# An attention stage that loads Q and K nine tokens to a partition, turns them with 64x64 products, and spreads its reciprocals by two transfers

## The chip, the cores and the metric

The kernel runs on one core of a Trainium2 chip. The metric is device time in microseconds (us) of one execution. The core has five engines that work side by side and meet through semaphores: PE (TensorE, the matrix engine; its loads of stationary operands are listed apart as PEld), DVE (VectorE), ACT (ScalarE), POOL (GpSimd) and SP (SyncE, which here only issues transfers). Transfers between DRAM and on-chip memory (DMAs) run on 16 DMA engines. Each engine takes its own instructions in the order in which the program wrote them.

## The reference

A forgetting attention over 4 batches of 8 heads, 576 tokens and 64 dimensions feeds two gated feed-forward layers.

```python
B, H, S, D = q.shape                       # 4, 8, 576, 64
scores = matmul(q, k^T) / sqrt(D)
cum    = cumsum(maximum(s, 0))             # one number per head and token
scores = where(causal, -1e9, scores + minimum(-(cum[i] - cum[j]), 0))
attn   = softmax(scores)                   # rows of 576 keys
x      = (attn @ v), heads joined          # 2304 tokens x 512
x      = (sigmoid(x @ w_gate) * (x @ w_val)) @ w_out      # 512 -> 1536 -> 512
h      = x @ w_in                                          # 512 -> 2048
out    = (h * cos(h)) @ w_out2                             # 2048 -> 512
```

The weights of the feed-forward layers come in 64-bit floats, which the kernel unpacks with integer operations into a high and a low 32-bit part (`wp`).

## The kernel before, in words

**Stages.** `attention()` handles 16 pairs of heads, `moe()` the two feed-forward layers. The attention leaves its result in `XH` and `XL` (a high and a low part). The feed-forward layers are three products for each one (`mm3`, lines 355 to 357) in an unbroken stream on PE, and `moe()` starts its own tiles in memory that the attention gave back, so its first gating waits for the attention's last user.

**One pair, p.** The names below are those of the order table.

- `GQp`, `GKp` (line 515) load Q and K. Two transfers per operand, one for each head: 512 of the 576 tokens, four tokens to a partition, written as 256-byte pieces. The last 64 tokens (the tail) of two pairs at a time come by `GQTp` (line 525, two transfers) and `GKTp` (line 522, one).
- `PQp`, `PKp` (line 546) turn the operand on PE: 10 transposes (5 slices x 2 heads, each 64 rows by 128 columns), into two PSUM banks `pw`. Q's tail is padded with zeros in the other head's half, so the score products of the tail can use all 128 columns.
- `HQp`, `HKp` (lines 433, 435, 437) copy the 640 columns from PSUM to `Q` or `K` in SBUF.
- `A3`, `A2`, `A0` (line 618) are the score products of the query tiles 3, 2 and 0 with 1; `A4` and `A5` (line 623) those of the tail, two turns that accumulate. The plan demands the order A4, A3 and A0, A2 and holds A5 back until the transposes T0 and T1.
- `X` (line 654, DVE) adds the bias and takes the row's extreme, `E` (line 658, ACT) the exponentials and their sums, `T` (line 444, PE) transposes the result, `C` copies it to `pt`, `V` (lines 728, 730) is the product with V into PSUM.
- `DBp` (line 554) spreads the pair's two cumulative sums over all 128 partitions (`CB`, 576 KB); `Z`, `ZT`, `ZA`, `ZM` on POOL mask it.
- `RA` (POOL), `RC` (DVE, line 740), `RT` (PE), `RR` (`rr`) make the reciprocals of the sums as rows; `RDp` (lines 749, 750) stores them to DRAM as `rec_d`; `RBp` (line 753) loads them back spread over 128 partitions, 64 for each head, into `rb` (288 KB). There is one `rb`, so the next RB waits for the division before it.
- `U` takes the product with V out of PSUM, `M` (line 759) multiplies by `rb`, `XH` and `XL` (line 771) split the result.

**What sets the order.** `SEQ` is one long table of those names, written out by hand or by a search; a suffix names the engine (`:a`, `:d`, `:p`). `plan.run` walks it once, and each engine gets its instructions in that order. The durations written beside each step only choose which of several buffers a step takes. All transfers but the first two are issued by SP, in the table's order; a transfer whose source or target isn't ready holds up those behind it.

The line that matters most here is the source of RB, whose first dimension is the pair's two heads:

```python
u.dma_start(out=RBT, in_=rec_d[p].unsqueeze(1).to_broadcast([2, 64, S]))
```

and that of DB, whose first dimension is the 128 partitions:

```python
u.dma_start(out=CB[cb.slot][:, :, 0:S], in_=cum_d[2 * p:2 * p + 2].unsqueeze(0).to_broadcast([P, 2, S]))
```

Of the kernel before, what the change touches and what calls it, by code (L numbers as in the profile page):

```python
# [10 lines left out]
F32 = mybir.dt.float32  # L11
# [78 lines left out]
MODE = {"V": 1, "warm": 2, "B": 2, "I": 2}  # L90
# [3 lines left out]
class Plan:  # L94
# [3 lines left out]
    def op(self, name, alts, rd=(), wr=(), needs=(), xfer=0.0, at=0.0):  # L98
# [3 lines left out]
        o.mode = MODE.get(re.match("[A-Za-z]*", name)[0], 0)  # L102
# [68 lines left out]
GQ0 cum tail B0 B1 GK0 GQT0 GKT0 out PQ0 table GK1 GQ1 BC0:d BC1:a Z0.0:p PK0 ZM0.3.0 HK0:a HQ0:d PK1 ZT0.0 Z1.0:a A3.0 DB1 ZT1.0 X0.3.0 ZA1.0 ZM1.3.0 ZA0.0 X1.3.0 HK1:a  # L171
PQ1 A4.0 ZM1.2.0 A0.0 GK2 A2.0 ZM0.2.0 HQ1:a ZT1.1 GK3 E0.3.0 GQ2 A4.1 X1.1.0 ZT0.1 X1.0.0 ZA1.1 X0.0.0 ZA0.1 Z1.1:p E1.3.0 Z0.1:p GQ3 X0.1.0 X1.2.0 ZM1.3.1 E1.1.0 X0.2.0
ZM0.3.1 E1.0.0 A0.1 E0.0.0 T0.0.0 E0.1.0 X1.0.1 T0.1.0 X1.1.1 X0.0.1 E1.2.0 X0.1.1 C0.1.0:d C0.0.0:a E0.1.1 A5.0 E0.0.1 A3.1 T0.3.0 GKT2 E1.0.1 X0.4.0 E1.1.1 T1.3.0 GQT2
T0.0.1 E0.4.0 X0.3.1 X1.3.1 T0.1.1 C0.0.1:a PK2 C0.3.0:a HK2:a ZM1.2.1 C1.3.0:d ZM0.2.1 A5.1 C0.1.1:d DB2 E0.2.0 T0.4.0 PQ2 ZT1.2 PK3 GV1 X0.4.1 A2.1 HQ2:a PQ3 GV0 E0.4.1
C0.4.0:d HQ3:a ZA1.2 T0.2.0 HK3:d ZT0.2 T1.2.0 A4.2 T0.4.1 X0.2.1 X1.2.1 A0.2 C0.4.1:d GQ4 ZA0.2 X1.0.2 C0.2.0:a Z1.2:p GQ6 X0.1.2 C1.2.0:a A3.2 E0.3.1 E1.3.1 E1.2.1 RA0
E1.0.2 T0.3.1 ZM1.3.2 X1.1.2 E0.1.2 Z0.2:p T1.3.1 X0.0.2 DB3 E0.2.1 X1.3.2 C1.3.1:a ZM0.3.2 C0.3.1:d RC0 GKT4 GK4 Z0.3:p V0.0 V1.0 T0.2.1 E0.0.2 X0.3.2 ZM1.2.2 E1.1.2
ZM0.3.3 T0.1.2 T0.0.2 T1.2.1 U0:a A5.2 Z1.3:p C0.0.2:d C0.2.1:d C0.1.2:a A2.2 C1.2.1:a ZT0.3 PK4 ZT1.3 A3.3 X0.4.2 X1.2.2 E0.3.2 GQT4 E1.3.2 ZM1.3.3 T0.3.2 ZM0.2.2 X0.2.2
HK4:a T1.3.2 GK5 ZA0.3 C1.3.2:a RT0 X0.3.3 E1.2.2 DB4 V0.1 ZM0.2.3 RR0:d V1.1 RA1 C0.3.2:d E0.4.2 T0.4.2 PQ4 X1.3.3 RC1 ZM1.2.3 RD0 ZA1.3 A4.3 U1:d HQ4:d GK6 A0.3 GV2
E0.2.2 ZT1.4 X1.0.3 X0.0.3 X0.1.3 E0.3.3 Z0.4:p E1.3.3 GV4 RT1 C0.4.2:a ZT0.4 RR1:a Z1.4:p ZA1.4 E1.0.3 E0.0.3 E0.1.3 A2.3 T0.2.2 ZA0.4 X1.1.3 T1.2.2 X0.2.3 A3.4 X1.2.3
RA2 E1.1.3 ZM1.3.4 C1.2.2:a RB0 T0.0.3 T0.1.3 A5.3 RC2 C0.0.3:a C0.2.2:d ZM0.3.4 C0.1.3:a PK5 RD1 HK5:a GQ5 X0.3.4 DB5 M0:p X0.4.3 warm0 RT2 T0.3.3 T1.3.3 RR2:d RB1  # L180
X1.3.4 A4.4 E0.4.3 C0.3.3:a C1.3.3:a ZM0.2.4 RD2 E1.2.3 T0.4.3 Z0.5:p A0.4 Z1.5:p E0.2.3 C0.4.3:d PQ5 X0.0.4 X1.0.4 X1.1.4 V0.2 GKT6 X0.1.4 V1.2 ZT1.5 HQ5:d T0.2.3 RA3
E1.0.4 ZT0.5 E1.3.4 XH0:p E1.1.4 E0.3.4 A2.4 E0.1.4 T1.2.3 U2:a E0.0.4 RC3 C1.2.3:a T0.1.4 C0.2.3:d X0.2.4 C0.1.4:a ZM0.3.5 T0.0.4 ZM1.2.4 A5.4 T0.3.4 GQT6 C0.0.4:a
X1.2.4 C0.3.4:a X0.4.4 T1.3.4 PQ6 HQ6:a C1.3.4:d A3.5 E0.4.4 RT3 GV3 PK6 RR3:d ZM1.3.5 X1.3.5 GK7 M1:p X0.3.5 ZA1.5 HK6:a ZA0.5 A4.5 DB6 E1.2.4 A0.5 X0.1.5 T0.4.4 XL0:p
E0.3.5 GK9 XH1:d V0.3 E0.2.4 X0.0.5 C0.4.4:d V1.3 E1.3.5 Z0.6:p E0.1.5 X1.0.5 RB2 T0.2.4 X1.1.5 E1.0.5 E0.0.5 A2.5 T1.2.4 ZT0.6 ZM1.2.5 ZT1.6 GQ7 U3:d ZM0.2.5 E1.1.5
X1.2.5 ZA1.6 ZA0.6 T0.0.5 RD3 T0.1.5 ZM0.3.6 X0.2.5 A5.5 M2:p C0.2.4:a C1.2.4:a T0.3.5 GV5 Z1.6:p RA4 C0.0.5:a T1.3.5 X0.4.5 C0.3.5:d GQ8 PQ7 C0.1.5:a PK7 DB7 HQ7:a
E0.4.5 C1.3.5:d A3.6 ZM1.3.6 A4.6 X0.3.6 X1.3.6 A0.6 HK7:a RC4 T0.4.5 X0.0.6 E0.3.6 XH2:p Z1.7:p ZM1.2.6 GQ10 ZT1.7 E1.3.6 V0.4 RB3 X1.0.6 E0.0.6 X1.1.6 GQT8 C0.4.5:d
V1.4 RT4 E0.2.5 Z0.7:p ZM1.3.7 E1.1.6 X0.1.6 E1.0.6 ZM0.2.6 XL2:d E1.2.5 A2.6 RR4:a T0.2.5 U4:d T0.0.6 E0.1.6 T1.2.5 C0.2.5:a ZM0.3.7 GK8 T0.1.6 A5.6 GKT8 C1.2.5:a T0.3.6
T1.3.6 ZT0.7 C0.1.6:a ZA1.7 X0.2.6 X1.2.6 PQ8 X0.4.6 C0.0.6:a E0.2.6 A3.7 C0.3.6:a ZA0.7 M3:p C1.3.6:a HQ8:d RD4 A4.7 E0.4.6 RA5 X0.3.7 E0.3.7 A0.7 X1.3.7 ZM1.2.7 X0.0.7
X0.1.7 X1.1.7 w0fetch DB8 X1.0.7 E0.1.7 PK8 E1.2.6 HK8:d E0.0.7 RB4 RC5 E1.3.7 w0exponent V0.5 XL1:p T0.4.6 RT5 RA6 GV6 RR5:a V1.5 C0.4.6:d T0.2.6 E1.1.7 ZT1.8 ZM0.2.7
E1.0.7 U5:a A2.7 T1.2.6 Z0.8:p w0mant_hi Z1.8:p C1.2.6:a GQ9 RC6 T0.0.7 C0.2.6:d T0.1.7 X1.2.7 A5.7 X0.2.7 C0.0.7:a PK9 RD5 C0.1.7:a A4.8 HK9:a T0.3.7 X0.4.7 XH3:p RT6  # L190
T1.3.7 ZT0.8 ZA1.8 GK10 M4:p RR6:a GV7 DB9 C0.3.7:a A0.8 C1.3.7:d PQ9 ZM0.3.8 E1.2.7 ZA0.8 RB5 HQ9:a A3.8 E0.4.7 ZM1.3.8 X1.0.8 XL3:p V0.6 X0.0.8 E0.0.8 X0.1.8 E0.2.7
X1.1.8 E1.1.8 E1.0.8 V1.6 w0mant_lo T0.2.7 X0.3.8 X1.3.8 GQT10 T0.0.8 T1.2.7 RA7 ZM0.2.8 E0.1.8 U6:d T0.1.8 E0.3.8 XH4:p C1.2.7:d C0.2.7:a C0.0.8:a A5.8 C0.1.8:a RC7
GKT10 T0.4.7 A2.8 X0.4.8 PQ10 C0.4.7:a A4.9 ZT1.9 HQ10:a ZT0.9 E1.3.8 ZA1.9 A0.9 ZM1.2.8 RT7 RD6 ZA0.9 GQ11 Z1.9:p X0.2.8 X1.2.8 X1.1.9 ZM1.3.9 Z0.9:p RR7:a E0.2.8 DB10
X0.1.9 X0.0.9 E1.2.8 A3.9 X1.0.9 ZM0.3.9 T0.3.8 E0.4.8 E0.0.9 X0.3.9 GK11 T1.3.8 C1.3.8:a M5:p X1.3.9 ZM1.2.9 V0.7 E0.1.9 T0.4.8 RA8 XH5:p XL4:p C0.3.8:d E1.0.9 T0.2.8
# [25 lines left out]
def kernel(  # L220
# [841 lines left out]
```

## Time and profile before

| what | us |
|---|---|
| median of 3 runs | 1095.63 (1095.25 to 1098.82) |
| the profiled execution | 1097.39 |
| its span, first to last instruction | 1095.5 |
| the stage up to 9 us: loads, warm-up, cumulative sums | 9.0 |
| the attention, 9 to 248 us | 239.0 |
| the feed-forward layers, 248 us to the end | 847.5 |

The boundaries were read from the timeline: the first transposes of Q start just before 9 us, and the first product after the gating waits until 248.0 us. In the profile, an engine's busy time says how much work there was; the idle time before an instruction, and what ended it, says what it waited for. An instruction that SP issues is short; what counts for a transfer is when somebody who needs it can start. PEclk is the share of TensorE's full clock (2.4 GHz) that was granted, 1.0 for 2.4 and 0.5 for 1.2 GHz.

### The profile page before, as it was taken

The numbers are of one execution on the slowest core, as the hardware profiler recorded it, in microseconds if no ns is written. First come the engines' busy times: TensorE is split into PE (matmuls) and PEld (weight loads), VectorE is DVE, ScalarE is ACT, GpSimd is POOL, SyncE is SP. The second block draws the span as 40 slices with busy tenths as digits, with TensorE's granted clock in tenths as the row PEclk, the third lists the DMA queues.
The fourth block names the chain that finished last, engine by engine and source line by source line (L and its number), as shares of the span: only waits on it lengthen the run. The fifth ranks groups of instructions, "written<-read, shape, count | busy, mean of one in ns | idle before, by whom it ended". The sixth has DMA issues, their size and how long they took to land.

```text
span 1095.5 us, 17441 instructions
## 1 busy us (share of the span) xinstructions
PE 1032.2 (94%) x6554; PEld 932.9 (85%) x6554; DVE 706.5 (64%) x1366; ACT 477.8 (44%) x1079; POOL 406.6 (37%) x484
## 2 busy tenths in 40 slices
PE   8778768859999999999999999999999999999998
PEld 5555445539999999999999999999999999999997
DVE  5656546536665564775434488898778978885664
ACT  5757657614422221222212134566555555555443
POOL 3345545424322122232111122465435545453222
PEclk9989888978999999999999999999999999999999
DMA  6645445303211111111101012111101101100111
GB/s 165 158 120 160 131 117 147 82 31 103 71 39 48 50 39 39 59 61 55 39 21 39 20 58 58 40 58 58 39 20 59 58 20 42 56 20 1 58 51 65
DMA packets 93668, 69.94 MB, mean 64 GB/s; under 512 B 61008, under 2 KB 81872, under 8 KB 93584
## 3 DMA queue, kind: packets, MB, share of 16 engines
q1 hardware_dynamic: 92192, 68.43, 21.6%
q8 instruction: 51, 0.84, 0.3%
q10 hardware_dynamic: 1392, 0.40, 0.2%
q14 instruction: 33, 0.27, 0.1%
HBM read 63.95 MB, written 4.87 MB: 63 GB/s over the span
## 4 chain that ended last, share of the span: by engine, by line
PE 77%; DVE 0%; ACT 0%; DVEq 0%; issue 0%
PE pw L356 20%; PE pw L355 20%; PE pw L357 20%; PE pw L909 6%; PE pw L911 6%; PE pw L910 6%; DVE acc L927 0%; ACT gh L829 0%; DVEq L1057 0%
## 5 line engine op out<-in xcount | busy, mean ns | idle before, releaser
L355 PE MATMUL pw<-XH,wp 128*128 128x384 f32 x960 | 322.9, 336 | 1.0 <-DVE w L437 1.0
L357 PE MATMUL pw<-XH,wp 128*128 128x384 f32 x960 | 322.7, 336 | 0.0
L356 PE MATMUL pw<-XL,wp 128*128 128x384 f32 x960 | 322.7, 336 | 0.0
L310 POOL TENSOR_TENSOR wp<-wm,wp 128x512 fp32r<-128x512 f32 x68 | 100.9, 1485 | 228.9 <-DVE wp L309 226.3
L355 PEld LDWEIGHTS pw<-XH,wp 128*128 128x128 f32 x960 | 180.3, 188 | 5.3 <-DVE w L437 1.1
L356 PEld LDWEIGHTS pw<-XL,wp 128*128 128x128 f32 x960 | 180.1, 188 | 3.6
L357 PEld LDWEIGHTS pw<-XH,wp 128*128 128x128 f32 x960 | 180.1, 188 | 0.0
L899 POOL TENSOR_TENSOR gl<-tm,gh 128x384 fp32r<-128x384 f32 x96 | 109.2, 1137 | 143.8 <-ACT gh L898 143.7
L302 POOL TENSOR_TENSOR wm<-wm,wx 128x512 int32<-128x512 int32 x68 | 90.3, 1328 | 188.6 <-DVE wm L301 182.3
L827 DVE TENSOR_TENSOR tm<-pw,tm 128x384 f32<-128x384 f32 x72 | 40.1, 557 | 150.7 <-PE pw L357 139.1
L909 PE MATMUL pw<-wp,gh 128*128 128x512 f32 x288 | 112.2, 389 | 0.0
L910 PE MATMUL pw<-wp,gh 128*128 128x512 f32 x288 | 112.1, 389 | 0.0
L911 PE MATMUL pw<-wp,gl 128*128 128x512 f32 x288 | 112.1, 389 | 0.0
L355 PE MATMUL pw<-gh,wp 128*128 128x384 f32 x288 | 97.5, 339 | 7.9 <-ACT gh L829 7.9
L884 DVE SCALAR_TENSOR_TENSOR tm<-tm 128x384 f32<-128x384 int32 x96 | 98.2, 1023 | 3.3
L829 ACT CAST gh<-tm 128x384 fp32r<-128x384 f32 x72 | 37.0, 514 | 140.8 <-DVE tm L827 139.9
L356 PE MATMUL pw<-gl,wp 128*128 128x384 f32 x288 | 97.8, 340 | 0.0
L885 ACT ACTIVATE tm<-tm 128x384 f32<-128x384 f32 x96 | 50.5, 526 | 108.0 <-DVE tm L884 108.0
L357 PE MATMUL pw<-gh,wp 128*128 128x384 f32 x288 | 96.9, 337 | 0.0
L289 ACT ACTIVATE wx<-wx,ebias 128x512 int32<-128x512 int32 x68 | 49.2, 723 | 105.5 <-DVE wx L288 104.3
L658 ACT ACTIVATE pu<-pu,nm 128x512 f32<-128x512 f32 (+4 forms) x144 | 83.0, 579 | 10.5 <-POOL pu L437 6.2
L826 ACT ACTIVATE tm<-pw 128x384 f32<-128x384 f32 x72 | 35.1, 487 | 111.8 <-PE pw L357 95.8
(100 smaller groups left out, 1673.4 us busy)
## 6 DMA issues: line engine op xcount, KB each, us to landing
raw<-in_moe_w_out_dram SPq DMA_DIRECT2D x28, 512.0 KB
CB<-cum_d SPq DMA_DIRECT2D x15, 576.0 KB
raw<-in_moe_w_in_dram SPq DMA_DIRECT2D x16, 512.0 KB
raw<-in_moe_w_gate_dram SPq DMA_DIRECT2D x12, 512.0 KB
raw<-in_moe_w_val_dram SPq DMA_DIRECT2D x12, 512.0 KB
VN<-in_v_dram SPq DMA_DIRECT2D x31, 160.0 KB
rb<-rec_d SPq DMA_DIRECT2D x16, 288.0 KB
out_dram<-acc SPq DMA_DIRECT2D x17, 256.0 KB
```

What stands on the lines that cost most here:

```text
L302: pool.tensor_tensor(m, m, st["x"], ALU.add)
L310: pool.tensor_tensor(w[:, 1], m, f(w[:, 0]), ALU.subtract)
L355: pe.matmul(ps, wh, xh, start=first, stop=False)
L356: pe.matmul(ps, wh, xl, start=False, stop=False)
L357: pe.matmul(ps, wl, xh, start=False, stop=last)
L658: act.activation(o, o, AF.Exp, bias=NMT[nm.slot][:, col:col + 1], scale=-1.0, accum_out=SUMS[sums.slot][:, col:col + 1])
L884: dve.scalar_tensor_tensor(r, kk, -TWO_PI_LO, r, ALU.mult, ALU.add)
L885: act.activation(r, r, AF.Sin, scale=0.5)
L899: pool.tensor_tensor(gl, g, f(gh), ALU.subtract)
L909: pe.matmul(ps, gh[:, ts], w[:, 0], start=it["first"], stop=False)
L910: pe.matmul(ps, gh[:, ts], w[:, 1], start=False, stop=False)
L911: pe.matmul(ps, gl[:, ts], w[:, 0], start=False, stop=it["last"])
```

## The change

- Q and K of a pair come in one transfer per operand: 576 tokens as 9 to a partition, 64 partitions to a head, 2304 bytes in one piece. The transfers of the tails are gone, with their tiles `QKT`.
- They are turned by plain products with the identity: 9 slices x 2 heads, each 64 rows by 64 columns, with the two heads on the two diagonal quarters of PE. A product of 32-bit floats is two records on PE, a transpose one.
- `H` copies 576 columns and writes them with a step of nine words, so that the tokens come in order.
- The tail's scores are four products of 64 rows by 64 columns, in one step A4; A5 is gone, and with it the order that the plan demanded among the A's. The last keys stand last, and `pu4` has 64 columns of zeros behind them.
- `RB` is two transfers, one for each head, each with 64 partitions as the first dimension of its source.
- `SEQ` is another table, in full.

```diff
-GQ0 cum tail B0 B1 GK0 GQT0 GKT0 out PQ0 table GK1 GQ1 BC0:d BC1:a Z0.0:p PK0 ZM0.3.0 HK0:a HQ0:d PK1 ZT0.0 Z1.0:a A3.0 DB1 ZT1.0 X0.3.0 ZA1.0 ZM1.3.0 ZA0.0 X1.3.0 HK1:a
+GK0 GK1 cum GQ0 PK0 B0 B1 table out BC0:a HK0:d GQ1 tail ZT0.0 PQ0 BC1:d Z1.0:p GK2 ZM1.3.0 ZT1.0 HQ0:a PK1 Z0.0:a DB1 PQ1 A4.0 X0.4.0 ZM0.3.0 A3.0 ZA0.0 HQ1:a ZA1.0 A0.0
...
-            QKN = {x: [att.tile([P, NT4, 2, D], F32, name=f"{x}n{i}") for i in range(NQK)] for x in "QK"}
-            QKT = {x: att.tile([P, 2, 2, D], F32, name=f"{x}t") for x in "QK"}
+            QKN = {x: [att.tile([P, S], F32, name=f"{x}n{i}") for i in range(NQK)] for x in "QK"}
...
-            PU.append([att.tile([P, S], F32, name=f"pu4{i}") for i in range(NPU[4])])
+            PU.append([att.tile([P, NQ * P], F32, name=f"pu4{i}") for i in range(NPU[4])])
...
-                for e in range(2):
-                    u.memset(QKT["Q"][half(1 - e), :, e], 0.0)
-                u.memset(QKT["K"][half(1)], 0.0)
+                for i in range(NPU[4]):
+                    u.memset(PU[4][i][:, S:NQ * P], 0.0)
...
-                        for e in range(2):
-                            u.dma_start(out=QKN[x][qk.slot][:, :, e], in_=src[e, 0:NT4 * P].rearrange("(p c) d -> p c d", c=NT4))
+                        u.dma_start(out=QKN[x][qk.slot], in_=src.rearrange("h (p c) d -> (h p) (c d)", c=NR))
...
-                        for c in range(NQ):
-                            for h in range(2):
...
-                                i = QKN[x][qk.slot][half(h), c] if c < NT4 else QKT[x][half(h), p % 2]
-                                pe.transpose(o, i.rearrange("p e d -> p (e d)"), ident[half(h), half(h)])
+                        for c in range(NR):
+                            for e in range(2):
+                                pe.matmul(wide(ps)[half(e), c * D:(c + 1) * D], QKN[x][qk.slot][half(e), c * D:(c + 1) * D], ident[half(e), half(e)], start=True, stop=True)
...
-                        copy(u, cols(x, OPS[x][cc.slot]), grid(x, ps), 0.125 if x == "Q" else 1.0)
+                        copy(u, OPS[x][cc.slot].rearrange("p (y c) -> p c y", c=NR), wide(ps).rearrange("p (c y) -> p c y", c=NR), 0.125 if x == "Q" else 1.0)
...
-                    def scores4(u, turn, sc=sc, cc=cc):
-                        for e in range(2):
-                            z = e ^ turn
-                            pe.matmul(PW[:, sc[0].slot + z, 0:HS], OPS["Q"][cc.slot][half(e), QCOL[NT4]:QCOL[NT4] + P], OPS["K"][cc.slot][half(e), z * HS:(z + 1) * HS], start=turn == 0, stop=turn == 1)
+                    def scores4(u, sc=sc, cc=cc):
+                        for z in range(2):
+                            for e in range(2):
+                                pe.matmul(PW[half(e), sc[0].slot + z, 0:HS], OPS["Q"][cc.slot][half(e), NT4 * P:S], OPS["K"][cc.slot][half(e), z * HS:(z + 1) * HS], start=True, stop=True)
...
-                    u.dma_start(out=RBT, in_=rec_d[p].unsqueeze(1).to_broadcast([2, 64, S]))
+                    for e in range(2):
+                        u.dma_start(out=RBT[half(e)], in_=rec_d[p, e].unsqueeze(0).to_broadcast([64, S]))
```

Two engines show what the new table and the new loads do. First SP in the middle of the attention, from the fourth spread `rb` to the fifth, before (names: `Qt`, `Kt` are the tails, `Qn`, `Kn` the four-token loads, `rec_d<-rr` the stored reciprocals, `raw` a piece of a weight):

```order
L753 DMA rb<-rec_d 128x1x576
L525 DMA Qt<-in_q_dram 64x2x64 x2
L515 DMA Kn_90<-in_k_dram 128x4x64 x2
L522 DMA Kt<-in_k_dram 64x4x64
L749 DMA rec_d<-rr 2x4x128
L750 DMA rec_d<-rr 2x1x64
L284 DMA raw<-in_moe_w_gate_dram 128x4x256
L554 DMA CB_83<-cum_d 128x2x576
L753 DMA rb<-rec_d 128x1x576
```

The same stretch, from the fourth spread to the fifth, after:

```order
L720 DMA rb<-rec_d 64x576 x2
L508 DMA Qn_87<-in_q_dram 128x576
L545 DMA VN_85<-in_v_dram 128x5x64 x2
L525 DMA CB_83<-cum_d 128x2x576
L715 DMA rec_d<-rr 2x4x128
L716 DMA rec_d<-rr 2x1x64
L508 DMA Kn_89<-in_k_dram 128x576
L284 DMA raw<-in_moe_w_gate_dram 128x4x256
L508 DMA Qn_88<-in_q_dram 128x576
L720 DMA rb<-rec_d 64x576 x2
```

The tails and the second halves of the loads are gone and the spread is two transfers; loads and the next stored reciprocals stand right behind a spread in both.

PE at the start of the second pair, before (`Kn0`, `Qn0` the loads, `pu` the exponentials that T transposes, `K1`, `Q1` the turned operands of the second pair):

```order
L546 MATMUL pw_121<-ident_78,Kn0_89 128x64 x8
L546 MATMUL pw_121<-ident_78,Kt_92 128x64 x2
L623 MATMUL pw_121<-K1_82,Q1_80 128x288 x2
L444 MATMUL pw_121<-ident_78,pu40_105 128x64 x10
L546 MATMUL pw_121<-ident_78,Qn0_87 128x64 x8
L546 MATMUL pw_121<-ident_78,Qt_91 128x64 x2
L546 MATMUL pw_121<-ident_78,Kn1_90 128x64 x8
L546 MATMUL pw_121<-ident_78,Kt_92 128x64 x2
L618 MATMUL pw_121<-K1_82,Q1_80 128x384 x2
```

After:

```order
L517 MATMUL pw_119<-ident_78,Kn0_89 64x64 x18
L443 MATMUL pw_119<-ident_78,pu30_100 128x64 x8
L443 MATMUL pw_119<-ident_78,pu31_101 128x64 x8
L588 MATMUL pw_119<-K1_82,Q1_80 128x512 x2
L593 MATMUL pw_119<-K1_82,Q1_80 64x288 x4
L517 MATMUL pw_119<-ident_78,Qn0_87 64x64 x18
L588 MATMUL pw_119<-K1_82,Q1_80 128x128 x2
```

An operand is 18 products of 64x64 where it was 10 transposes, the tail's scores are one block of four products, and blocks of the 64x64 form now stand between blocks of the 64-row form. Over the whole attention PE changes between forms of operand some 40 times before and some 80 times after.

## Rows read from the trace of the kernel before

**Rows 1.** Busy time by stretch: us, busy (instructions) per engine, PEclk, DMA share, GB/s.

```profile
9.00:195.00 186.00, 148.15 (x1703) 98.57 (x1704) 107.14 (x348) 125.69 (x373) 92.12 (x217) 0.90 0.55 142
195.00:248.00 53.00, 33.31 (x280) 22.37 (x276) 23.27 (x56) 18.05 (x47) 19.58 (x29) 0.85 0.19 51
248.00:1095.50 847.50, 843.71 (x4560) 808.62 (x4560) 572.61 (x955) 332.52 (x658) 292.16 (x226) 1.00 0.15 47
```

**Rows 2.** PE's waits, 9 to 249 us: for whom, us in total, times, longest.

```profile
PE pw L355 <- ACT gh L829: 7.9, 1, 7.9
PE pw L546 <- DMA Qt<-in_q_dram: 7.1, 2, 4.3
PE pw L444 <- DVE rc L740: 5.8, 1, 5.8
PE pw L728 <- DMA VN<-in_v_dram: 5.5, 4, 2.9
PE pw L444 <- DVE rr L437: 5.1, 1, 5.1
PE pw L444 <- ACT rr L433: 4.8, 2, 4.6
PE pw L546 <- DMA Qn<-in_q_dram: 4.7, 1, 4.7
```

**Rows 3.** Timeline, all engines, 106 to 119 us: start, us, engine, what, idle before.

```profile
106.55 0.55 SPq L753 DMA_DIRECT2D rb<-rec_d  x1
...
107.14 1.29 SPq L525 DMA_DIRECT2D Qt<-in_q_dram  x2
...
117.85 1.40 POOL L759 TENSOR_TENSOR w<-w,rb 128x576 f32<-128x576 f32 x1 [1.75 <-DMA rb<-rec_d]
118.02 0.57 PE L546 MATMUL pw<-ident,Qt 64*128 64x64 f32 x2 [4.27 <-DMA Qt<-in_q_dram]
```

**Rows 4.** The same view at the attention's end.

```profile
214.82 0.50 SPq L753 DMA_DIRECT2D rb<-rec_d  x1
...
223.34 1.40 POOL L759 TENSOR_TENSOR w<-w,rb 128x576 f32<-128x576 f32 x1 [8.54 <-DMA rb<-rec_d]
224.77 0.50 SPq L753 DMA_DIRECT2D rb<-rec_d  x1
...
233.63 0.50 SPq L753 DMA_DIRECT2D rb<-rec_d  x1
...
242.02 0.76 DVE L759 TENSOR_TENSOR w<-w,rb 128x576 f32<-128x576 f32 x1 [5.39 <-DMA rb<-rec_d]
...
248.00 0.69 PE L355 MATMUL pw<-gh,wp 128*128 128x384 f32 x1 [7.86 <-ACT gh L829]
```

**Rows 5.** The same view at a spread of CB, its issue and its first user.

```profile
29.02 0.37 SPq L554 DMA_DIRECT2D CB<-cum_d  x1
...
34.43 0.60 POOL L437 COPY pu<-CB 64x512 f32<-64x512 f32 x1 [5.59 <-DMA CB<-cum_d]
```

**Rows 6.** Sizes of the two spreads: issues, KB each.

```profile
CB<-cum_d SPq DMA_DIRECT2D x15, 576.0 KB
...
rb<-rec_d SPq DMA_DIRECT2D x16, 288.0 KB
```

**Rows 7.** Timeline of PE: transposes, then products of 64 columns (94 us); a long run of transposes.

```profile
94.45 0.28 PE L546 MATMUL pw<-ident,Kt 64*128 64x64 f32 x2
...
94.67 0.34 PE L728 MATMUL pw<-pt,VN 128*64 128x64 f32 x4
...
94.83 1.78 PE L730 MATMUL pw<-pt,VN 128*64 128x512 f32 x8
...
217.78 1.41 PE L444 MATMUL pw<-ident,pu 64*128 64x64 f32 x38 [1.11 <-ACT pu L658]
```

**Rows 8.** Copies out of PSUM by ACT, attention: count, busy us, mean ns, idle before.

```profile
L433 ACT ACTIVATE Q<-pw 128x640 f32<-128x640 f32 x11 | 7.8, 705 | 22.4 <-PE pw L546 22.4
...
L433 ACT COPY w<-pw 128x576 f32<-128x576 f32 x5 | 3.1, 628 | 0.9 <-PE pw L730 0.9
```

More of the change, by code (lines that the diff above doesn't have):

```diff
@@ L89 @@
 LAT = {"pe": 0.24, "act": 0.16, "dve": 0.13, "pool": 0.08}
[L90 removed]
+MODE = {"V": 1, "warm": 2, "B": 2, "I": 2, "PQ": 3, "PK": 3}
 SWITCH = 0.15
@@ L101, in op @@
         o.n, o.unit, o.start, o.end, o.ready = len(self.ops), None, None, None, at
-        o.mode = MODE.get(re.match("[A-Za-z]*", name)[0], 0)
+        o.mode = 3 if name[:2] == "A4" else MODE.get(re.match("[A-Za-z]*", name)[0], 0)
         deps = set()
@@ L216 @@
+RT15 V0.14 V1.14 V0.15 U14:d V1.15 RR15:a w2mant_hi M14:d w2mant_lo RD15 XL13:d XH14:a U15:a RB15 w2sign M15:d w2split XL10:d XL14:p XH15:p XL15:p
 """
@@ L242 @@
     NQ = 5
+    NR = 9
     TAIL = S - 4 * P
@@ L447, in attention @@
             zero = PU[4][1].bitcast(BF16)[:, 0:512]
-            ss, cs, one = WT[0][0:NH], WT[1][0:NH], PU[4][0][0:NH]
+            ss, cs, one = WT[0][0:NH], WT[1][0:NH], PU[4][0][0:NH, 0:S]
             sp.dma_start(out=ss, in_=s.rearrange("b h s -> (b h) s"))
@@ new lines, in load, with wide, prep @@
+                        u.dma_start(out=QKN[x][qk.slot], in_=src.rearrange("h (p c) d -> (h p) (c d)", c=NR))
+                    add(f"G{x}{p}", {"act" if p == 0 and x == "Q" else "sp": 0.62}, load, wr=[qk], xfer=0.8, at=0.72 if x == "Q" else 1.2)
+                    def wide(ps):
+                        return PW[:, ps.slot:ps.slot + 2].rearrange("p a x -> p (a x)")[:, 0:S]
+                    def prep(u, x=x, qk=qk, ps=ps):
+                        for c in range(NR):
+                            for e in range(2):
+                                pe.matmul(wide(ps)[half(e), c * D:(c + 1) * D], QKN[x][qk.slot][half(e), c * D:(c + 1) * D], ident[half(e), half(e)], start=True, stop=True)
@@ L549, in keep @@
+                    add(f"P{x}{p}", "pe:500", prep, rd=[qk], wr=[ps])
                     def keep(u, x=x, ps=ps, cc=cc):
-                        copy(u, cols(x, OPS[x][cc.slot]), grid(x, ps), 0.125 if x == "Q" else 1.0)
-                    add(f"H{x}{p}", "act:597 dve:800" if x == "Q" else "act:580 dve:740", keep, rd=[ps, "table"], wr=[(cc, x)])
+                        copy(u, OPS[x][cc.slot].rearrange("p (y c) -> p c y", c=NR), wide(ps).rearrange("p (c y) -> p c y", c=NR), 0.125 if x == "Q" else 1.0)
@@ L553, in spread_cum @@
+                    add(f"H{x}{p}", "act:540 dve:720" if x == "Q" else "act:525 dve:670", keep, rd=[ps, "table"], wr=[(cc, x)])
                 def spread_cum(u, cb=cb, p=p):
@@ L605, in at @@
                         x = PU[t][pu_of[t, e].slot]
-                        return x if t == NT4 else x[:, e * n:(e + 1) * n] if t < 2 else x
+                        return x[:, 0:S] if t == NT4 else x[:, e * n:(e + 1) * n] if t < 2 else x
                     def bias(t, e, cb=cb):
@@ L691, in transp @@
                                     for c in range(t + 1):
-                                        i = (TAIL + c * P) % S if t == NT4 else c * P
+                                        i = c * P
                                         flip(o, e * (t + 1) * 64 + c * 64, x[:, i:i + P])
@@ L711, in attention @@
                             src = [(sums, 2 * NT4)] if s4 else [(sums, t + NT4 * z) for z in es]
-                            add(f"T{e}.{t}.{p}", f"pe:{tT}", transp, rd=[pu, *[(pu, z) for z in es], *src], wr=[(tps, t, e), ("t01", p, t)], needs=[pt])
+                            add(f"T{e}.{t}.{p}", f"pe:{tT}", transp, rd=[pu, *[(pu, z) for z in es], *src], wr=[(tps, t, e)], needs=[pt])
                             add(f"C{e}.{t}.{p}", f"act:{tH} dve:{tD}", pt_copy, rd=[(tps, t, e), "tail"], wr=[(pt, z, t) for z in es])
@@ L765, in attention @@
                 add(f"RD{p}", {"sp": 1.35}, store_r, rd=[rr], wr=[("rec", p)], xfer=0.1)
-                add(f"RB{p}", {"sp": 0.62}, spread, rd=[("rec", p)], wr=[rb], xfer=0.9)
+                add(f"RB{p}", {"sp": 1.2}, spread, rd=[("rec", p)], wr=[rb], xfer=0.9)
                 add(f"U{p}", "act:520 dve:670", pv_out, rd=[ov], wr=[w])
```

136 lines of the change are left out of this document (51 added, 85 removed).

## Prediction

> **What bounds the kernel now.** I read the stretches first, then PE's waits, then the timeline around the long ones. The feed-forward layers fill 847.5 us with PE 843.7 us busy [rows 1]. The change doesn't touch their instructions, so I leave them as they are. All that can move lies between 9 and 248 us. There no engine is full: from 9 to 195 us PE is busy 148 of 186 us, ACT 126, DVE 107, POOL 92, and from 195 to 248 us PE only 33 of 53 [rows 1]. So waits set this stage, and the next view says which. PE's seven costliest waits come to 40.9 us [rows 2], and four of these lines name a transfer or the `rr` row, which waits for a stored transfer to land.
>
> The timeline shows where such a wait begins [rows 3]. At 106.55 SP issues a spread `rb`; POOL's division that needs it starts at 117.85. The tail of Q, issued at 107.14 right behind it, also arrives only at 118.02, after PE has waited 4.27 us for 32 KB. The same pattern stands at the end [rows 4]: a spread issued at 214.82 is used at 223.34, one issued at 233.63 at 242.02. That is 8.5 us from issue to use. CB, spread from DRAM in the same manner but with twice the bytes [rows 6], is used 5.4 us after its issue, by an engine that stood waiting for it [rows 5]. So `rb` takes far longer than its size explains, and what stands behind it on SP arrives with it. At the end the spreads even run in series: one `rb` buffer, so issue, 8.5 us, 1.40 us of division, next issue, 9.95 us in all [rows 4].
>
> What differs between the two sources is their first dimension: 2 heads for `rb`, 128 partitions for CB. The Trainium skill, page "DMA: Bandwidth & Descriptors", section "Rules for kernel authors", says that a leading broadcast of c copies, c under 16, confines a transfer to at most c of the 16 DMA engines. By that rule the new source (64 first) uses all 16; the trace's 8.5 against 5.4 us for half the bytes agrees.
>
> **The change part by part.** The sum stands against the profiled execution, 1097.4 us; the median of the runs is 1.8 us below it.
>
> *The end, 195 to 248 us.* The split spread lands sooner: from above its price is CB's 5.4 us [rows 5]; below lies nothing shorter than half of that for half the bytes, 2.7. I take 3.4, nearer to the half since the bytes are half: 5.1 us less per spread. A hop is then 4.8 us in place of 9.95, and the spreads no longer set the pace. Next late is PE's own work, 33.3 us [rows 1], with the chain behind the last division, 242.02 to 248.00, 6.0 us [rows 4]: 39.3 us for 53.0, a gain of 13.7. Bounds: 5.1 (only the last landing) and 19.7 (53.0 less 33.3).
>
> *Waits before 195 us.* Of rows 2 the tails of Q (7.1), the loads of Q (4.7), the two `rr` lines (5.1 and 4.8) and V (5.5, of which some 2 fall after 195 us) come to 25 us. The longest single one is 5.1, no more than a spread now loses, so each can vanish; but something else is late next each time (a product, a copy). I take three quarters, 19; bounds 10 and 25.
>
> *The clock.* PEclk is 0.90 in these 186 us [rows 1]: with 1.2 and 2.4 GHz the only levels, a fifth of the time is at 1.2, and a fifth of 148 us busy is 30, of which full clock would return 15. The lower level follows the waits. I take a third, 5; bounds 0 and 10.
>
> *Turning Q and K.* Two transposes alone, one for each head, take 0.28 us, and 38 take 1.41 [rows 7]: 18 pairs more in 1.13 us, 63 ns a pair. Ten were 0.31 us. The new form is nine pairs of products. The nearest row is the two products of V with 64 columns: four records from 94.67 to 94.83, 0.16 us [rows 7], the upper end; two records where a transpose has one, 0.126, is the lower. I take 0.13, since inside a block each weight load hides behind the product before: 1.17 us, so 0.86 more per operand; 32 operands, +27.5 us of PE work (bounds 26 and 36). With the waits gone PE would be busy 148 of 167 us, too full to hide it all and too empty to show it all: half, +14 (bounds 0 and 36).
>
> *Changes of form on PE.* From the first of two transposes at 94.45 to the first product of the other form at 94.67 are 0.22 us [rows 7]; less 0.063 for the pair, 0.15. Some 40 changes more: +6 at most, 0 at least; I take +3.5.
>
> *Tail scores, zeros, order of the A's.* Four products of 288 columns before and after; the two heads still run side by side. The zeros are cleared once. I cost these at nothing; what hides the clearing is the first loads' flight. If the four shared less, 0.3 us a pair, +5, which the bounds above hold.
>
> *H.* 640 columns took ACT 0.705 us; 576 take 0.628 in the copy of U [rows 8]. 32 copies are 2.5 us of ACT and DVE work less, off the path: 0. No row here writes with a step of nine words. Bounds: the 2.5 us less, and a doubling, +0.63 on each of 32, 20 us on two engines, a third on the path: +7.
>
> *Loads.* Q and K were 64 transfers with 24 tails, and now are 32; the spreads are 16 more. SP loses 40 issues net of 0.5 to 0.6 us [rows 3, 4]. The waits that this ends are counted above: 0, down to -5. The division now waits for two landings; POOL's masks and the next pair's reciprocals stand behind it there, as they do before, and SP has one more issue (0.5 us) ahead of the loads behind a spread.
>
> Sum: -13.7 - 19 - 5 + 14 + 3.5 + 0 = -20.2, so 1077.2 against the profiled execution and **1075 us** against the median. The far ends of all terms are -60 and +34, which won't meet.
>
> **The rivals.** *PE hides the turning.* The added PE work falls into the waits that stay: the two PE terms go to 0, 1075 - 17.5 = 1057.5. For it: 38 of 186 us without PE work. Against: PE's blocks must come in order.
>
> *PE becomes the bound (slower).* The place is PE in the stretch 9 to 195 us. 18 products where 10 transposes were, at 0.16 a pair, and 80 changes of form in place of 40, all on the path: +36 + 6, with the lower gains -5 (end), -10 (waits), 0 (clock): +27 on 1097.4, 1122.6 against the median. It decides once the added work on the path is above the 38 us of gains taken above. For it: PE is already the fullest engine [rows 1]. Against: a quarter of the stage is wait.
>
> *The spread doesn't get faster.* If the two halves run one behind the other, each at today's rate, `rb` lands at 8.5 us as before; only the lighter loads help, -5 by their bound, against +17.5: 1108. The row against it is CB's [rows 5]. The Trainium skill, same page and section, advises against two transfers to the two halves of the partitions, since both use the same 16 engines one after the other; by that rule the split gains nothing against one good transfer, and the trace's 8.5 us says that this one isn't good.
>
> *Strided writes cost.* H doubles, +7: 1082. The Trainium skill, page "SBUF — State Buffer", section "Door 1: The DMA port swizzle (why `[64,N]` ≈ `[32,N]`)", says that an access that enters a new 16-byte line each time pays a penalty; a step of 36 bytes does. No row here shows it.
>
> *Gains and costs cancel.* Half the end, half the waits, all of the turning: about 1095.
>
> **How the numbers follow.** Forecast 1075 (1062 to 1090 with its middle bounds): 0.60. PE hides the turning, 1057: 0.18. Strided writes, 1082: 0.05. PE the bound, 1122: 0.09. No faster spread, 1108: 0.05. Cancel: 0.03. A measurement of this kernel tells some 0.3% (3.3 us) from no change. Faster: 0.60 + 0.18 + 0.05 = 0.83; same 0.03; slower 0.09 + 0.05 = 0.14. The range of 1048 to 1094 leaves out the two slower cases and the cancelled one (0.17 together), and about 0.03 at the far end of the hidden case.
>
> **What would show each step.** Spread: the wait for `rb` before the division falls from 8.5 us to 2 to 3, and spreads at the end no longer stand 10 us apart. Waits: PE's lines for DMA and for `rr` fall from 27 us to under 8. Clock: PEclk in the attention rises from 0.89 to 0.95. Turning: 36 records in 1.1 to 1.4 us at full clock. H: 0.63 us on ACT; 1.2 shows the penalty. The attention should end near 226 us in place of 248, and the stretch behind it stay at 847 us. I am wrong if PE is over 90% busy in the attention with no long waits and the end is still near 248, or if new waits of 3 us and more stand before the new table's steps.

## The result and the profile after

| kernel | median, us | runs | ratio to before (95%) |
|---|---|---|---|
| before, on the same chip | 1096.89 | 1095.25 to 1098.82 | |
| changed | 1049.73 | 1047.53 to 1053.27 | 0.957 (0.954 to 0.961) |

The change gains 47 us. The forecast was 1075 us, a gain of 20.6: the sign was right, the size was less than half. The profiled execution took 1051.18 us, its span 1049.4.

First the stretches, as in [rows 1] (us, busy and instructions for PE, PEld, DVE, ACT and POOL, granted clock, DMA share, GB/s):

```profile
9.00:150.00 141.00, 136.68 (x2237) 94.68 (x2238) 102.16 (x319) 111.04 (x310) 85.58 (x203) 0.98 0.59 167
150.00:201.88 51.88, 44.16 (x545) 30.47 (x544) 33.00 (x94) 33.53 (x96) 31.99 (x49) 1.00 0.37 99
201.88:1049.40 847.52, 843.53 (x4560) 808.04 (x4560) 573.59 (x955) 332.72 (x658) 292.48 (x226) 1.00 0.15 47
```

The feed-forward layers are what they were, 847.5 us. The attention ends at 201.88 where it ended at 248.00, so all 46 us are there. Before, PE was busy 148 of the first 186 us of the attention [rows 1]; now it is busy 137 of the first 141, and the granted clock is 0.98 and 1.00, so 2.4 GHz nearly throughout. The list of PE's waits, 9 to 203 us (for whom, us in total, times, longest), holds no transfer, where [rows 2] had three in its first seven. Its first five of nine:

```profile
PE pw L355 <- ACT gh L796: 4.2, 1, 4.2
PE pw L443 <- ACT pt L432: 1.9, 2, 1.0
PE pw L355 <- ACT w L432: 1.3, 1, 1.3
PE pw L593 <- ACT w L432: 1.2, 1, 1.2
PE pw L443 <- DVE pt L436: 0.9, 1, 0.9
...
```

The timeline at the attention's end answers [rows 4]:

```profile
186.51 1.13 SPq L720 DMA_DIRECT2D rb<-rec_d  x2
...
190.38 0.76 DVE L726 TENSOR_TENSOR w<-w,rb 128x576 f32<-128x576 f32 x1
...
191.16 1.13 SPq L720 DMA_DIRECT2D rb<-rec_d  x2
...
194.92 0.76 DVE L726 TENSOR_TENSOR w<-w,rb 128x576 f32<-128x576 f32 x1 [1.91 <-DMA rb<-rec_d]
...
201.88 0.69 PE L355 MATMUL pw<-gh,wp 128*128 128x384 f32 x1 [4.21 <-ACT gh L796]
```

From issue to use is 3.8 us (191.16 to 194.92) instead of 8.5, and one spread follows the other after 4.65 us instead of 9.95. Part of that is the division between them, which DVE now does in 0.76 us and POOL did in 1.40 [rows 4].

Two more groups, by shape (count, busy us, mean ns, idle before), answer [rows 7] and [rows 8]: the products that turn an operand, and the copies H.

```profile
L517 PE MATMUL pw<-ident,Qn 64*64 64x64 f32 x576 | 21.1, 228 | 0.6 <-ACT K L432 0.5
L517 PE MATMUL pw<-ident,Kn 64*64 64x64 f32 x576 | 20.8, 225 | 1.0 <-DMA Kn<-in_k_dram 1.0
...
L432 ACT COPY K<-pw 128x576 f32<-128x576 f32 x9 | 10.9, 1214 | 2.9 <-PE pw L517 2.9
...
L436 DVE COPY K<-pw 128x576 f32<-128x576 f32 x7 | 8.4, 1204 | 3.4 <-PE pw L517 3.2
...
L436 DVE COPY w<-pw 128x576 f32<-128x576 f32 x8 | 6.0, 755 | 3.6 <-PE pw L696 3.6
...
L432 ACT COPY w<-pw 128x576 f32<-128x576 f32 x8 | 5.1, 632 | 2.4 <-PE pw L696 1.7 <-DVE XL L738 0.7
```

An H of 576 columns takes 1.21 us on ACT. A copy of as many columns without the step of nine words takes 0.63. (The 1.0 us for a load of K lies before the attention: the list of PE's waits, which starts at 9 us, doesn't have it.)

### The profile page after: what moved, and what is told of

It is laid out like the page before. It is cut to its first block, busy times and chain, and to the rows that moved or that the text cites. A ratio compares the mean times of both kernels' runs of the same rounds, so it can differ in the third digit from the quotient of the medians.

```text
span 1049.4 us, 19070 instructions
## 1 busy us (share of the span) xinstructions
PE 1031.2 (98%) x7386; PEld 936.9 (89%) x7386; DVE 712.6 (68%) x1374; ACT 479.4 (46%) x1066; POOL 411.5 (39%) x488
## 4 chain that ended last, share of the span: by engine, by line
PE 81%; DMA 1%; DVE 1%; POOL 0%; ACT 0%; SPq 0%; issue 0%; DVEq 0%; POOLq 0%
PE pw L356 20%; PE pw L355 20%; PE pw L357 20%; PE pw L876 6%; PE pw L878 6%; PE pw L877 6%; DMA rb<-rec_d 1%; PE pw L696 0%; PE pw L588 0%; PE pw L443 0%; DMA raw<-in_moe_w_gate_dram 0%; POOL XL L738 0%; DMA rec_d<-rr 0%; PE pw L593 0%; DVE acc L894 0%; POOL wp L310 0%
## 5 line engine op out<-in xcount | busy, mean ns | idle before, releaser
L626 ACT ACTIVATE pu<-pu,nm 128x384 f32<-128x384 f32 (+4 forms) x144 | 82.9, 581 | 2.9 <-DVE nm L622 2.8
L859 DVE SCALAR_TENSOR_TENSOR tm<-tm,pw 128x384 f32<-128x384 f32 x96 | 52.8, 550 | 42.8 <-ACT tm L853 42.8
```

What stands on the lines that cost most here:

```text
L626: act.activation(o, o, AF.Exp, bias=NMT[nm.slot][:, col:col + 1], scale=-1.0, accum_out=SUMS[sums.slot][:, col:col + 1])
L859: dve.scalar_tensor_tensor(g, r, -0.5, h, ALU.add, ALU.mult)
```

## The spread alone, put back and put in

The theory: the first dimension of the old source, 2, let a spread run on few DMA engines, and PE's waits and the cold clock both came from that one transfer. The rival: the lighter loads and the new table made the gain. The first run puts the old spread back into the changed kernel.

```diff
-                    for e in range(2):
-                        u.dma_start(out=RBT[half(e)], in_=rec_d[p, e].unsqueeze(0).to_broadcast([64, S]))
+                    u.dma_start(out=RBT, in_=rec_d[p].unsqueeze(1).to_broadcast([2, 64, S]))
```

> The changed kernel, with only its spread of the reciprocals put back into one transfer whose source leads with the two heads. Theory (that spread's shape made the waits, and the cold clock with them): PE's waits on transfers and on the stored reciprocals come back, 30 to 50 us of them, an issue of the spread is used some 8 us later at the end of the attention, and the time goes from 1050 back to 1080 to 1110 us; over 1096 would mean that the rest of the change costs time by itself. Rival (the lighter loads of Q and K and the new table made the gain): 1050 to 1058 us, and PE still waits for little.

The second puts the new spread, and nothing else, into the kernel before (the same diff the other way round).

> The kernel before, with only its spread of the reciprocals split into two transfers, one for each head. Theory (the spread's shape made the waits): most of the 58 us in which PE stands still in the attention goes, without the 22 us of added turning, so the time falls from 1096 to between 1035 and 1060 us, and may beat the changed kernel. Rival (loads and table made the gain): 1085 to 1097 us, only the last landings are earlier.

Measured on one chip, before at 1097.55 us: 1084.07 (1080.20 to 1084.43) for the first, **1040.69** (1039.76 to 1046.13) for the second. Both times lie where the theory put them, and far from the rival's.

| median, us | spread in one | spread by heads | the spread is worth |
|---|---|---|---|
| old loads, turning, table | 1097.55 | 1040.69 | 56.9 |
| new loads, turning, table | 1084.07 | 1049.73 | 34.3 |
| the rest is worth | 13.5 | **-9.0** | |

(The changed kernel's 1049.73 is from another chip, where before took 1096.89.) The spread makes more than the whole gain. The rest of the change gains while the spread is slow, and loses once it is fast. That the changed kernel is the slower of the two good ones was then measured on one chip, the changed kernel as it is beside the second kernel once more:

> The changed kernel as it is, beside the kernel before with the split spread alone, on one chip. Theory (the turning of 64x64 products costs more than the lighter loads give once the spread is good): the changed kernel is the slower of the two by 5 to 12 us, at 1047 to 1052 us. Rival (the difference of 9 us between 1050 and 1041 came from the chips that they ran on): the two lie within 3 us of each other.

> The kernel before with only its spread split by heads, beside the changed kernel on one chip. Theory: 1038 to 1044 us, 5 to 12 us under the changed kernel, with the first gated product at 190 to 197 us. Rival: within 3 us of the changed kernel.

1052.66 us (1052.23 to 1053.13) and 1041.87 (1036.61 to 1043.07): 10.8 us apart, at the far end of what the theory gave. The kernel before, with only the spread's two lines from the changed kernel, beats the changed kernel.

The rows show why the spread is worth so much. The view of the tile `rb` says how long its users, the divisions, stood before it (us, times), in all and then for one of the two engines that divide. First the kernel before:

```profile
  DMA rb<-rec_d: 59.7, 13
...
  POOL w L759: 54.3, 12
```

the same in the changed kernel:

```profile
  DMA rb<-rec_d: 2.1, 2
...
  DVE w L726: 1.9, 1
```

and in the changed kernel with the old spread:

```profile
  DMA rb<-rec_d: 49.6, 15
...
  POOL w L725: 37.0, 12
```

In the kernel before, POOL stood for 54 of 239 us at its division, and by the order of the program its masks and sums for the next pairs stand behind that in its queue. With the split spread alone (the run beside the changed kernel) the divisions wait 11.8 us for `rb`, and PE's list names no transfer any more. With the old spread in the changed kernel, PE waits for a transfer and for a stored reciprocal again (waits of PE):

```profile
...
PE pw L443 <- DVE pt L436: 5.4, 3, 4.0
PE pw L517 <- DMA Kn<-in_k_dram: 5.1, 1, 5.1
PE pw L443 <- ACT rr L432: 5.0, 1, 5.0
...
```

These are fewer than the 30 to 50 us that were written: PE's idle time up to the first gated product rises from 12.0 to 32.3 us. The rest of the way back is clock: 12.5 us more busy time for the same instructions (the two rows stand in the section on PE's work, below).

## How many engines a spread uses

Is it the first dimension, or only that there are two transfers? The next kernel is the one before with two transfers by halves of the columns, each source still led by the two heads:

```diff
-                    u.dma_start(out=RBT, in_=rec_d[p].unsqueeze(1).to_broadcast([2, 64, S]))
+                    for z in range(2):
+                        zc = slice(z * HS, (z + 1) * HS)
+                        u.dma_start(out=RBT[:, zc], in_=rec_d[p, :, zc].unsqueeze(1).to_broadcast([2, 64, HS]))
```

> The kernel before, with its spread also split into two transfers, but by halves of the columns, so that each source still leads with the two heads. Theory (the first dimension of 2 decides): no gain, 1090 to 1100 us, and a spread is used some 8 us after its issue as before. Rival (two transfers run side by side, whatever their shape): the same time as with the split by heads.

1105.72 us (1105.21 to 1107.51), ratio 1.008 (1.005 to 1.010): slightly slower than before, a little beyond the theory's 1100, and the division's waits for `rb` are 65.6 us. The rival falls. Then the split by heads with a source that leads with 4:

```diff
-                        u.dma_start(out=RBT[half(e)], in_=rec_d[p, e].unsqueeze(0).to_broadcast([64, S]))
+                        u.dma_start(out=RBT[half(e)], in_=rec_d[p, e].unsqueeze(0).unsqueeze(0).to_broadcast([4, 16, S]))
```

> The kernel before, with its spread split into two transfers, one for each head, as in the run that gave 1041 us, but each source written as 4 times 16 copies, so that it leads with 4 and not with 64. Theory (the first dimension of the source sets how many of the 16 DMA engines move it): the one transfer that leads with 2 moves 46 GB/s before, so these move some 92 GB/s, one behind the other 3.1 us for 288 KB where the one takes 6.3; the landing lies between 3.9 and 8.5 us, and the time between the two, 1050 to 1075 us. Rival (two transfers with halves of the partitions are enough): 1037 to 1046 us. Rival (any small first dimension is as bad as 2): 1090 to 1100 us.

1064.34 us (1062.71 to 1066.57): between the two, as the theory put it, with 32.7 us of waits for `rb`. The rates stand in the stretches in which hardly anything but a spread moves (last two columns: share of the 16 DMA engines, GB/s). In the kernel before, led by 2:

```profile
227.00:232.50 5.50, 5.50 (x28) 2.29 (x26) 3.76 (x7) 1.87 (x2) 0.31 (x1) 0.55 0.13 47
```

led by 4:

```profile
203.30:206.30 3.00, 3.00 (x19) 2.91 (x17) 0.00 (x0) 0.00 (x0) 1.05 (x1) 1.00 0.23 75
```

and in the changed kernel, led by 64:

```profile
192.70:194.40 1.70, 1.19 (x7) 1.19 (x8) 0.31 (x1) 1.68 (x2) 1.22 (x1) 1.00 0.58 163
```

0.13 is two of 16 engines, 0.23 nearly four; the last is a mean over a burst that starts and ends inside the stretch. The Trainium skill, page "DMA: Bandwidth & Descriptors", section "Rules for kernel authors", says that an outermost dimension below 16 confines a transfer to at most as many engines; 0.13 and 0.23 agree. The same section's advice against two transfers to the two halves of the partitions takes it that either way uses all 16 engines; the one transfer replaced here used two, and the two that replace it are worth 34 to 57 us.

## Does the added PE work lie on the path?

The changed kernel with every operand turned twice, then the same with the old spread:

```diff
-                        for c in range(NR):
+                        for c in [*range(NR), *range(NR)]:
```

> The changed kernel, with the 18 small products that turn an operand issued twice, everything else alike; the second set overwrites the first with the same values. It adds 32 times 1.2 us, 38 us of PE work. Theory (PE is now the bound of the attention, so that all of the turning lies on the path): 1050 goes to 1083 to 1090 us. The forecast's own view (half of it hides): 1066 to 1072 us. Rival (PE hides the turning): under 1060 us.

> The changed kernel with its spread in one transfer again (1084 us), and with the 18 products that turn an operand issued twice, 38 us of PE work more; the second set overwrites the first with the same values. With the good spread the same doubling cost 31 us. Theory (what the turning costs depends on the waits: beside a slow spread PE stands still and the work hides in that): under 19 us, 1090 to 1103 us. Rival (PE's blocks come in order, so that work adds whatever else waits): 1110 to 1122 us.

With the good spread 1081.14 us (1078.84 to 1081.65), 31.4 more than the changed kernel's 1049.73 and 28 more than its 1052.66 and 1052.81, all from other chips. The stretches up to the first gated product, changed kernel first:

```profile
9.00:201.88 192.88, 180.84 (x2778) 125.15 (x2777) 135.16 (x412) 144.57 (x405) 117.57 (x251) 0.99 0.53 149
```

```profile
9.00:231.09 222.09, 212.35 (x3901) 156.55 (x3901) 136.81 (x413) 145.72 (x406) 117.87 (x252) 1.00 0.47 132
```

PE is busy 31.5 us longer and the stretch is 29.2 longer. The added work was less than the 38 us that I had put on it (0.98 us an operand against 1.23 for a first set, it seems because a second set follows a first in the same form), but what there is of it lies on the path, 29.2 of 31.5 us. I read that as the theory holding with its price mis-sized; 1081 is just outside what was written for it. It tells what work costs that is added to the changed kernel, whose PE is already full, and not what the first set cost when it came in.

With the old spread 1104.55 us (1101.02 to 1107.09), 20.5 more than 1084.07, which is from another chip (19.2 when each is taken against before on its own chip). Its stretch beside that of the kernel it is compared with, which ends at 234.62:

```profile
9.00:234.62 225.62, 193.34 (x2782) 132.12 (x2781) 135.66 (x412) 145.31 (x406) 117.79 (x252) 0.95 0.45 129
```

```profile
9.00:252.54 243.54, 220.37 (x3904) 161.33 (x3900) 136.16 (x413) 146.22 (x406) 117.82 (x252) 0.96 0.43 120
```

27.0 us more busy, 17.9 more time: a third hides in PE's idle time, which falls from 32 to 23 us. 20.5 lies between what the two sides had written (under 19, 26 to 38), so neither range was met; the theory holds in direction, with less cover than I gave it: what the turning costs depends on the waits beside it.

## Where the 13 us came from

With the old spread the rest of the change gained 13.5 us in spite of the turning. One run splits the loads of Q and K by heads again, under the old spread:

```diff
-                        u.dma_start(out=QKN[x][qk.slot], in_=src.rearrange("h (p c) d -> (h p) (c d)", c=NR))
+                        for e in range(2):
+                            u.dma_start(out=QKN[x][qk.slot][half(e)], in_=src[e].rearrange("(p c) d -> p (c d)", c=NR))
```

> The changed kernel with its spread in one transfer again (1084 us), and with the loads of Q and K split in two, one for each head, 32 issues more. With that spread the rest of the change was worth 13 us in spite of 22 us of added turning, and this asks where they came from. Theory (fewer transfers stand in the queue behind a slow spread): 1090 to 1100 us. Rival (the new table, or the loads' nine tokens in one piece, did it): 1080 to 1088 us.

1093.74 us (1091.11 to 1095.70), 9.7 more than 1084.07 (8.4 when each is taken against before on its own chip). Beside a slow spread the number of transfers costs; the division's waits rise from 49.6 to 62.2 us. The rest of the gain, the missing tails and the new table, was not tested apart, nor was what the lighter loads are worth beside a fast spread.

## The copies H

The same copies, written without a step in SBUF and read with a step of 64 words in PSUM:

```diff
-                        copy(u, OPS[x][cc.slot].rearrange("p (y c) -> p c y", c=NR), wide(ps).rearrange("p (c y) -> p c y", c=NR), 0.125 if x == "Q" else 1.0)
+                        copy(u, OPS[x][cc.slot].rearrange("p (y c) -> p y c", c=NR), wide(ps).rearrange("p (c y) -> p y c", c=NR), 0.125 if x == "Q" else 1.0)
```

> The changed kernel, with only the copies of the turned operands changed: they write their 576 columns of SBUF one after the other and take the step of 64 words on the side of PSUM. If it is the step of nine words in SBUF that doubles these copies, ACT's fall from 1.21 to 0.63 us and DVE's from 1.21 to 0.76; if a step on either side does it, they stay at 1.2. For the time: theory (PE is the bound, ACT and DVE have room) no change, 1044 to 1052 us. Rival (the longer copies hold PE up, as the 7 us that the forecast put on a doubling): 1036 to 1044 us.

```profile
L432 ACT COPY K<-pw 128x576 f32<-128x576 f32 x9 | 5.7, 637 | 4.0 <-PE pw L517 4.0
...
L436 DVE COPY K<-pw 128x576 f32<-128x576 f32 x7 | 5.3, 756 | 3.5 <-PE pw L517 3.5
```

The copies are 0.64 and 0.76 us, so it is the step in SBUF that makes them longer, by a factor of 1.9 on ACT and 1.6 on DVE. The Trainium skill, page "SBUF — State Buffer", section "Door 1: The DMA port swizzle (why `[64,N]` ≈ `[32,N]`)", says that an access which enters another 16-byte line each time pays a penalty; a step of 36 bytes does, and 1214 ns against 637 agrees. The time was 1046.96 us (1046.42 to 1049.86), a ratio of 0.953 (0.951 to 0.956) on its chip. Against the changed kernel's 0.957 on one chip and 0.961 on the other that left open whether the copies or the chips differ, so the two ran side by side, with no other edit:

> The changed kernel as it is, as the partner of the next run on the same chip. Theory (PE is the bound, the doubled copies H have room beside it): within 3 us of the kernel with the contiguous copies. Rival (the doubled copies hold PE up, as the 7 us put on them): 4 to 8 us slower than it.

> The changed kernel with the copies H writing SBUF without a step, beside the changed kernel as it is. Theory: within 3 us of it, 1047 to 1052 us. Rival: 4 to 8 us faster than it, 1042 to 1047 us.

1052.81 us (1052.56 to 1053.18) as it is, 1051.22 (1049.48 to 1052.27) with the contiguous copies: 1.6 us. That is less than the 4.3 us by which the same contiguous kernel differs between this run and the one above, on one chip. The doubled copies are real, and no cost of theirs is clear of that scatter; ACT is busy 145 and DVE 135 of the 193 us of the attention, so both have room beside PE's 181.

## The tail's scores alone

If PE is the bound, its lighter tail scores should pay in the better kernel too: the kernel before with the spread by heads and four products in A4, A5 taken out of the table.

```diff
-                    def scores4(u, turn, sc=sc, cc=cc):
-                        for e in range(2):
-                            z = e ^ turn
-                            pe.matmul(PW[:, sc[0].slot + z, 0:HS], OPS["Q"][cc.slot][half(e), QCOL[NT4]:QCOL[NT4] + P], OPS["K"][cc.slot][half(e), z * HS:(z + 1) * HS], start=turn == 0, stop=turn == 1)
+                    def scores4(u, sc=sc, cc=cc):
+                        for z in range(2):
+                            for e in range(2):
+                                pe.matmul(PW[half(e), sc[0].slot + z, 0:HS], OPS["Q"][cc.slot][half(e), QCOL[NT4] + e * TAIL:QCOL[NT4] + (e + 1) * TAIL], OPS["K"][cc.slot][half(e), z * HS:(z + 1) * HS], start=True, stop=True)
```

> The kernel before with its spread split by heads (1041 us), and with the tail's scores also taken from the changed kernel: four products of 64 rows by 64 columns in the step A4 in place of two turns with 128 columns, A5 gone, everything else in the old table's order. The old form has PE busy 24.5 us for 128 records, the new one 18.8 in the changed kernel. Theory (PE is the bound once the waits are gone, so its work counts): 5.7 us less, against up to 4.8 for two more changes of form per pair: 1034 to 1040 us, faster than both kernels. Rival (the order now sets the end, or the changes of form eat it): 1040 to 1046 us.

1048.36 us (1047.11 to 1050.61), a ratio of 0.956 (0.954 to 0.958) where the spread by heads alone gave 0.949 and 0.951: some 6 us slower for the edit. The theory falls. The rows of the tail's products, without the edit and then with it:

```profile
L623 PE MATMUL pw<-K,Q 64*128 64x288 f32 x128 | 23.9, 450 | 1.2 <-DVE nm L654 0.4 <-DVE pt L437 0.4 <-DVE K L437 0.3
```

```profile
L623 PE MATMUL pw<-K,Q 64*64 64x288 f32 x128 | 19.7, 429 | 3.8 <-DVE nm L652 2.4 <-DVE pt L437 0.8 <-ACT pt L433 0.3
```

They are 4.2 us shorter and wait 2.6 us longer, and PE's busy time over the attention doesn't fall (165.11 us up to 193.22; 167.20 up to 198.50). No other line's records grow by more than 1 us, so what is lost seems to be overlap between one block and the next. Why was not settled: the changes of form, now two more for each pair, are one candidate, and the old table's order, which was made for two turns, is another.

## Why the forecast missed, step by step

The kernel before with the split spread alone has the same instructions on PE as the kernel before, so the difference in PE's busy time between them is the clock. Before, in the stretch to the first gated product:

```profile
9.00:248.00 239.00, 181.46 (x1980) 120.93 (x1980) 130.41 (x404) 143.74 (x419) 111.70 (x245) 0.89 0.47 122
```

with the split spread alone (the run beside the changed kernel):

```profile
9.00:193.22 184.22, 165.11 (x1982) 109.17 (x1981) 128.73 (x404) 143.35 (x419) 111.17 (x246) 0.99 0.60 156
```

The same kernel, cut where PE has done 1703 instructions, as many as the kernel before has done at 195 us [rows 1]:

```profile
9.00:158.00 149.00, 136.32 (x1703) 89.41 (x1704) 106.32 (x348) 125.02 (x372) 91.39 (x218) 0.99 0.68 175
158.00:193.22 35.22, 28.79 (x281) 19.76 (x277) 22.41 (x56) 18.33 (x48) 19.79 (x29) 1.00 0.28 76
```

| part, us | forecast | by the split spread alone | by the rest | together |
|---|---|---|---|---|
| PE's waits, the end | -13.7 | -13.3 (19.7 idle to 6.4) | | |
| PE's waits before it | -19 | -25.2 (37.9 idle to 12.7) | | |
| PE's waits in all | -32.7 | -38.4 | -7.1 | -45.5 |
| clock | -5 | -16.4 (181.46 to 165.11 busy) | | -16.4 |
| PE's own work | +14 + 3.5 = +17.5 | 0 | +15.7 (165.11 to 180.84 busy) | +15.7 |
| the attention's end | -20.2 | -54.8 | +8.7 | -46.1 |

Of the 26 us between forecast and result, 11.4 are the clock, 6.2 the waits before the end, and 8.8 are the rest of the change, which lengthened the attention by 8.7 us where its PE terms said 17.5.

**The spread: right.** 3.8 us from issue to use where 3.4 was taken, by the rule on the first dimension, as the runs led by 4 and by column halves show. The end's waits came out at 13.3 us for 13.7. That a hop is 4.65 us where 4.8 was forecast is partly luck: the forecast had POOL's division of 1.40 us in it, and the one measured has DVE's of 0.76.

**The waits before the end: mis-sized.** The lines of PE that name a transfer or `rr`, five of them and not the four of the prediction's opening, come to 25 us. The forecast kept three quarters because something else would be late next each time. As much as all of those lines went, 25.2 us. POOL's 54.3 us before its divisions were a row that I had not read: PE's list says what came last, the tile's says what held up the rest.

**The clock: mis-sized, and the worst miss.** For the stretch before the end the forecast worked out 15 us for full clock and then took a third of it; 11.8 came (148.15 to 136.32). The end, at 0.85 [rows 1], had no clock term, and gave 4.5 more (33.31 to 28.79). The granted clock is 0.99 where it was 0.89, in the kernel in which nothing but the spread differs. Having written that the lower level follows the waits, I should have scaled the clock with the waits that go, not by a second, smaller share.

**The turning: the work was a little less than forecast, and what of it lies on the path is not shown apart.** The stretches of its lines, with the split spread alone and in the changed kernel:

```profile
9.00:193.22 184.22, 16.27 (x320) 13.96 (x320) 0.99 0.60 156
```

```profile
9.00:201.88 192.88, 39.21 (x1116) 37.10 (x1116) 0.99 0.53 149
```

22.9 us more, where 27.5 was forecast. The new form takes 1.23 us an operand, near the 1.17 forecast; ten transposes take 0.51 and not 0.31. The forecast took each of five pairs at 0.063 us; with 0.28 for the first, as two transposes alone take [rows 7], its own rows give 0.53. The tail's scores, costed at nothing, are shorter in the changed kernel (18.8 us against 23.9). So PE's busy time grew by 15.7 us; that this lies near the +17.5 is luck, since that sum took only half of the turning. From the kernel with the split spread alone to the changed one the attention is 8.7 us longer and PE's idle time falls from 19.1 to 12.0 us. So about half of the added work shows, as the forecast assumed, but loads and table differ between the two as well, and no run has the new turning without them. What is added on top of the changed kernel is paid nearly in full, as the run that turned twice shows, and two thirds of it beside the old spread.

**H: the rival's mechanism was true, its price wasn't.** The doubling had a chance of 0.05 and happened, to 1.21 us; the +7 put on it was 1.6 side by side, not clear of the scatter.

**Loads:** 0 to -5 was not tested beside a fast spread; beside the slow one 32 issues cost 8 to 10.

**The rivals.** *PE hides the turning* gave 1057, the nearest time, and for a reason that is at most half true. *PE becomes the bound* was right that PE fills up, and wrong that this makes the kernel slower: it decided, by the forecast, above 38 us of gains, and the spread alone gave 54.8. The cancelled rival's 1095 holds only with the forecast's 17.5 us for PE; with all of the turning, as its words have it, its sum is near 1107. The signs named ahead were right in kind: waits for transfers and `rr` 27 to under 8 (1.5, all for `rr`), the clock from 0.89 to 0.95 (0.99), the end near 226 (201.88).

## What to carry to other kernels

Look at the first dimension of a spread's source before looking at its bytes, and ask the tile's view who stands before it: a slow transfer shows in the queues of engines that are not the bound. When waits go, take the clock with them, and then price what is added to an engine that has become full at nearly its whole cost. Test the parts of a change apart: here two lines were worth 57 us, and the rest, which gained 13 beside the fault, lost 9 to 11 without it.

## What the hardware showed that I had not expected

- A small first dimension shows directly as a share of the 16 DMA engines, in a stretch in which little but a spread moves: 2 gave 0.13 and 47 GB/s, 4 gave 0.23 and 75. Cutting such a transfer by columns made the kernel 8 us slower.
- A step of nine 32-bit words on the SBUF side makes a copy 1.9 times as long on ACT (637 to 1214 ns) and 1.6 times on DVE (756 to 1204); a step of 64 words on the PSUM side costs nothing (ACT 637 ns against 632 without any, DVE 756 against 755).
- Four products in place of two turns, each record shorter, did not lower PE's busy time in the old order.
